# Turning the attention probabilities and half of the LN2 output without TensorE in a DiT block

## The chip, the core and the metric

The kernel runs on one core of a Trainium2 chip. The metric is the device time of one execution in microseconds (us): the median of three runs of the kernel before is 243.12 us (242.97 to 244.42). Engines are named as the profile names them: PE (TensorE, matmuls), PEld (its weight loads), DVE (VectorE), ACT (ScalarE), POOL (GpSimd) and SP (SyncE, which issues most of the DMAs).

## The reference

One block of a diffusion transformer on x of shape (2, 256, 1152), with a modulation vector c of shape (2, 1152), two heads of 576, and a hidden width of 4608, all in bf16:

```python
mod = (silu(c) @ w_mod).reshape(B, 6, 1, D)
shift_a, scale_a, gate_a, shift_m, scale_m, gate_m = [mod[:, i] for i in range(6)]
h = layernorm(x) * (1 + scale_a) + shift_a
q, k, v = split(h @ wqkv)
attn = softmax(einsum('bqhd,bkhd->bhqk', q, k) * Dh ** (-0.5))
x = x + gate_a * (einsum('bhqk,bkhd->bqhd', attn, v).reshape(B, N, D) @ wo)
h2 = layernorm(x) * (1 + scale_m) + shift_m
return x + gate_m * (gelu(h2 @ w_fc1) @ w_fc2)
```

## The kernel before, in words

The 512 tokens are four tiles of 128 (t = 0, 1 for the first batch, 2, 3 for the second); the 1152 features are nine chunks of 128. Weights stream in from DRAM by large DMAs issued on SP. The SBUF is one hand-made arena, and buffers are used again: the four fc1 buffers `WFC1` (512 hidden columns each, so four tiles f) are filled a second time, and the end of the `WFC2` area holds the normalised tiles `XN2` for a while.

Every operation is recorded as a unit with its reads and writes (class `Sched`). Dependencies follow from the regions. The order on PE and on SP is the order in which the code records the units; the order on ACT, DVE and POOL is made by a list scheduler with a cost model (`schedule`), unless `S.first` or `order_after` says otherwise. Each engine then runs its list strictly in order, and an instruction that waits on a semaphore holds up all that stands behind it on that engine. That holds for SP and POOL as issuers of DMAs too.

Stages on PE in order: the modulation columns, k, then q; the scores S of each batch and head, with softmax on DVE and ACT (`s_and_softmax`: maximum, exp with the sum beside it, reciprocal, and a multiplication on DVE at L1013 that normalises the probabilities `PP`); between the v projections (`v_proj`, PSUM banks 0 to 2 in turn) the probabilities are turned (`pt_transposes`: four 128x128 transposes for each batch and head into PSUM, and one copy to `PTS`); `rows` (modulation rows); PV (`pv_halves` for the chunk that the two heads share, then `pv`) into `OT`; the output projection `wo_tile` of t = 0 to 3, with gate, residual and the statistics of LN2. The gate itself is a chain on DVE (`attn_gate`, 18 long operations at L1061 and L1064, run wherever DVE is free) that goes through DRAM (`dit_scratch`).

LN2 gives `XN2[t]`, token-major. `xn2_T(t)` turns it by nine PE transposes into PSUM, from where DVE and ACT write it with scale and shift to `H2T`, feature-major. Then fc1: for the first F0 = 9 of its 36 tiles f, the 256 tokens of batch 0 are computed first (half tiles of nine matmuls of 256 columns), with `xn2_T(2)` after f = 3 and `xn2_T(3)` after f = 6; then the same nine tiles for batch 1; from f = 9 on tiles of 512 columns. ACT applies gelu (L1200). At f = 16, 20, ... the reloaded fc1 quarters are first used. fc2 follows, 13 pieces, each stored as it is done.

SP's order from PV on is: GA loads, fc1 quarters 2 and 3, `WGM` (2592 KB, for the MLP gate), WFC2 parts 1, 2 and 3 (2592 KB each; part 3 must wait until `XN2` has been read), fc1 quarters 4 to 8 (1152 KB each, number 4 needs the buffer of quarter 0 free), WFC2 part 0, output stores.

```python
seq = {e: [u for u in units if u.eng == e] for e in ("pe", "sp")}
...
for f in range(F0, JT):
    if f % 4 == 0 and f // 4 >= 4:
        wfc1_load(f // 4)
    fc1_tile(f, 0, 512)
```

Of the kernel before, what the change touches and what calls it, by code (L numbers as in the profile page):

```python
# [9 lines left out]
SEM_LAT = 120.0  # L10
# [161 lines left out]
class Sched:  # L172
    def __init__(self):
        self.units = []
        self.instrs = []
        self.sb_recs = {}
        self.sb_buckets = defaultdict(set)
        self.bank_pe = defaultdict(list)
        self.bank_other = defaultdict(list)
        self.bank_prev_other = defaultdict(list)  # L180
        self.cur_unit = None
        self.first = {}

# [21 lines left out]

# [75 lines left out]
    def schedule(self, dma_bw=385.0, dma_issue=650.0, dma_lat0=900.0, dma_lat1=600.0, verbose=False):  # L281
# [44 lines left out]
        while scheduled < n:  # L326
# [39 lines left out]
            for f, uid in fin_now:  # L366
                for s in units[uid].succ:
                    ndeps[s.uid] -= 1
                    at = max(avail_time.get(s.uid, 0.0), f + (SEM_LAT if True else 0.0))
# [139 lines left out]
F0 = 9  # L509
# [34 lines left out]
def build_kernel(nc, x, c, wqkv, wo, w_mod, w_fc1, w_fc2, out):  # L544
# [4 lines left out]
    scratch = scratch_t.ap()  # L549
    with (  # L550
# [442 lines left out]
        def s_and_softmax(b, h):  # L993
            idx = b * 2 + h
            bank = s_bank[(b, h)]
            S.unit("pe", 8 * c_mm(256), "S_%d_%d" % (b, h))
            ch = head_chunks[h]
            for jq in range(2):
                for ci, (gq, gk) in enumerate(ch):
                    q0 = b * 256 + jq * 128  # L1000
                    mm(ps32(bank, jq * 256, 256), QK[:, gq, q0:q0 + 128], QK[:, gk, b * 256:(b + 1) * 256], False, ci == len(ch) - 1,
                       skip_group_check=True)
            s3 = ps32(bank).rearrange("p (j k) -> p j k", j=2)
            mx, nb, rsum, ri, pp = MX[:, idx, :], NB[:, idx, :], RS[:, idx, :], RI[:, idx, :], PP[idx]
# [7 lines left out]
            rib = ri.unsqueeze(2).broadcast_to([P, 2, 256])  # L1012
            u = dve(c_dve_tt16(512), lambda e: e.tensor_tensor(out=pp, in0=pp, in1=rib, op=ALU.mult), [pp, ri], [pp], "spn_%d" % idx)  # L1013
            if idx % 2 == 1:
                S.order_after(ga_units[(1, 7) if idx == 1 else (0, 8)], u)

        def pt_transposes(b, h):
            idx = b * 2 + h
            bank = s_bank[(b, h)]
            S.unit("pe", 4 * c_mm(128), "PT_%d_%d" % (b, h))  # L1020
            for kjt in range(2):
                for jq in range(2):
                    tr(ps16(bank, kjt * 256 + jq * 128, 128), PP[idx][:, jq, kjt * 128:(kjt + 1) * 128], IDENT)
            copy_on("dve" if b == 0 else "act", PTS[idx].rearrange("p j k -> p (j k)"), ps16(bank, 0, 512), 512, True, "PT_ev%d" % idx)

        v_banks = [0, 1, 2]
        v_rr = [0]

        def v_proj(t, ci):
            bank = v_banks[v_rr[0] % 3]  # L1030
# [87 lines left out]
        PVB = [(6, 7, 0, 1), (3, 4, 0, 1)]  # L1118

        def pv_halves():  # L1120
            S.unit("pe", 4 * c_mm(256) + 100.0, "PV_halves")
            for b in range(2):
                for kjt in range(2):
                    for h in range(2):
                        f0 = 512 + 64 * h
                        mm(psum[64 * h:64 * h + 64, 5 * 512 + b * 256:5 * 512 + b * 256 + 256], V[:, 2 * b + kjt, f0:f0 + 64],
                           PTS[b * 2 + h][:, kjt, :], b == 0 and kjt == 0, b == 1 and kjt == 1, skip_group_check=True,
                           tile_position=(0, 64 * h))
            S.order_after(copy_on("dve", OT[:, 4, :], ps32(5), 512, False, "OT_ev_4"), last_mt[0])

        def pv(b, h):
# [3 lines left out]
            for g in range(g0, g0 + 4):  # L1135
                bank, half = PVB[b][2 * h + (g - g0) // 2], (g - g0) % 2
                for kjt in range(2):
                    mm(ps32(bank, half * 256, 256), V[:, 2 * b + kjt, g * 128:(g + 1) * 128], PTS[idx][:, kjt, :], kjt == 0, kjt == 1)
            tok = slice(b * 256, (b + 1) * 256)
            for i, eng in ((0, "act"), (1, "dve")):  # L1140
# [12 lines left out]
        def wo_tile(t, before={}):  # L1153
            b = t // 2
            for ci in range(NCH):
# [4 lines left out]
                for g in range(KT):  # L1160
                    mm(o, OT[:, g, t * 128:(t + 1) * 128], WO[:, g, ci * CH:(ci + 1) * CH], g == 0, g == KT - 1)
# [13 lines left out]
        def xn2_T(t):  # L1175
# [7 lines left out]
            for kt in range(KT):  # L1183
                o, dst = slot[kt], H2T[:, kt, t * 128:(t + 1) * 128]
                s1, s2 = SC1M[:, kt * 2 + b:kt * 2 + b + 1], SHM[:, kt * 32 + b:kt * 32 + b + 1]
                if kt < (4 if t < 2 else 6):
# [5 lines left out]

        def fc1_tile(f, tok0, ntok):
# [3 lines left out]
            for kt in range(KT):  # L1197
                mm(o, WFC1[q % 4][:, kt, (f % 4) * 128:(f % 4) * 128 + 128], H2T[:, kt, tok0:tok0 + ntok], kt == 0, kt == KT - 1)
# [23 lines left out]
        pt_transposes(0, 0)  # L1222
        v_proj(1, 0)
        pt_transposes(1, 0)
        v_proj(1, 1)
        v_proj(1, 2)
        pt_transposes(0, 1)
        v_proj(2, 0)
        v_proj(2, 1)
        pt_transposes(1, 1)  # L1230
# [63 lines left out]
        S.n_other_dma_sems = 12  # L1294
# [3 lines left out]
        with ExitStack() as es:  # L1298
            sems = {e: es.enter_context(nc.semaphore("c_" + e)) for e in ENGINES}
            dma_sems = [es.enter_context(nc.semaphore("d%d" % i)) for i in range(60)]  # L1300
# [47 lines left out]
```

## Time and profile before

| what | before |
|---|---|
| median of the timed runs | 243.12 us |
| span of the profiled execution (first to last instruction) | 242.5 us |
| the same execution's own time | the page gives its span alone; the median of the timed runs is 0.6 us longer |
| PE busy | 237.3 us (98%) |
| DVE, ACT, POOL busy | 121.5, 67.8, 19.9 us |
| moved by DMA | 51.58 MB, mean 213 GB/s |

How to read it: the span runs from the first to the last instruction of one profiled execution, and all places in time below are microseconds from its start. The rows of forty digits cut the span into slices of 6.06 us; a digit is a busy share in tenths, and the row PEclk is the clock that TensorE was granted. Matmuls are pipelined and their ends are modelled, so a busy PE in a slice does not mean that it never waited; the chain of waits and the regular distance of the gelu starts (0.98 us for a half tile, 1.94 us for a tile of 512) say that. The landing time of a DMA runs from its issue on SP to its last byte, and holds the time that it stood behind others.

### The profile page before, as it was taken

The page shows a single profiled execution, that of the slowest core. Times are in us where ns is not written, and L with a number is a line of the kernel's source. Part 1 is how long each engine was busy: PE and PEld are TensorE (multiplying, and loading weights), DVE is VectorE, ACT ScalarE, POOL GpSimd, SP SyncE. Part 2 cuts the span into 40 slices and gives each one's busy share as a digit, 9 for nine tenths or more (in the row PEclk, how much of TensorE's full clock was granted, in tenths as well). Part 3 has the DMA queues.
Part 4 walks back from the last instruction along what each step waited for, and adds up shares of the span by engine and source line. Part 5 has one row for each costly group of instructions (what it writes and reads, how often), then busy time and mean ns, then how long its engine had stood idle before and what let it go on. Part 6 is the DMA issues. An engine that isn't in the chain of part 4 may idle for free.

```text
span 242.5 us, 3957 instructions
## 1 busy us (share of the span) xinstructions
PE 237.3 (98%) x1699; PEld 145.4 (60%) x1699; DVE 121.5 (50%) x229; ACT 67.8 (28%) x136; POOL 19.9 (8%) x36
## 2 busy tenths in 40 slices
PE   6899999999999999999999999999999999999995
PEld 2688844466666666898544444444666566566564
DVE  2654379988996689669999700000022222111112
ACT  4921440435524206973233322222000000000000
POOL 1300000000002276400000110000000000000000
PEclk9979999999999999999999999999999999999999
DMA  6999999999992999999963499100000000000000
GB/s 221 378 370 392 389 392 390 398 413 402 391 352 79 312 374 391 391 348 398 352 198 83 157 313 374 43 0 3 0 16 19 16 16 16 19 16 16 21 27 20
DMA packets 30363, 51.58 MB, mean 213 GB/s; under 512 B 1547, under 2 KB 15755, under 8 KB 30347
## 3 DMA queue, kind: packets, MB, share of 16 engines
q1 hardware_dynamic: 29888, 50.73, 58.9%
q0 software_dynamic: 288, 0.60, 0.8%
q8 instruction: 13, 0.21, 0.4%
q10 hardware_dynamic: 171, 0.01, 0.0%
q14 instruction: 3, 0.02, 0.0%
HBM read 50.15 MB, written 1.19 MB: 212 GB/s over the span
## 4 chain that ended last, share of the span: by engine, by line
PE 95%; DMA 3%; SPq 1%; DVE 0%; issue 0%
PE psum L692 93%; DMA arena<-in_wqkv_dram 3%; PE psum L695 2%; SPq L673 1%; DVE arena L1290 0%; DVE arena L1291 0%
## 5 line engine op out<-in xcount | busy, mean ns | idle before, releaser
L692 PE MATMUL psum<-arena 128*128 128x384 bf16 (+8 forms) x1610 | 234.0, 314 | 2.4 <-POOL arena L718 1.5
L692 PEld LDWEIGHTS psum<-arena 128*128 128x128 bf16 (+2 forms) x1610 | 139.7, 97 | 92.4 <-issue 3.8
L1290 DVE TENSOR_TENSOR arena<-psum,arena 128x384 f32<-128x384 f32 (+2 forms) x13 | 6.8, 526 | 88.6 <-PE psum L692 88.6
L1200 ACT ACTIVATE arena<-psum 128x512 bf16<-128x512 f32 (+1 forms) x45 | 22.8, 512 | 42.1 <-PE psum L692 42.1
L687 ACT ACTIVATE arena<-psum 128x512 bf16<-128x512 f32 (+6 forms) x34 | 18.2, 560 | 37.9 <-PE psum L692 37.9
L1064 DVE SCALAR_TENSOR_TENSOR arena<-arena 128x1152 f32<-128x1152 bf16 x16 | 21.9, 1408 | 0.0
L1095 DVE SCALAR_TENSOR_TENSOR arena<-arena 128x1152 f32<-128x1152 bf16 x16 | 21.4, 1414 | 0.0
L1166 POOL TENSOR_TENSOR arena<-arena 128x384 f32<-128x384 f32 x12 | 10.9, 912 | 11.7 <-DVE arena L1165 9.5
L740 DVE BATCH_NORM_STATS2 arena<-arena 128x6 f32<-128x384 f32 (+1 forms) x18 | 9.5, 549 | 3.8 <-DMA arena<-in_x_dram 3.8
L673 POOL DMA_DIRECT2D dit_scratch<-arena x4 | 2.4, 609 | 96.6 <-DVE arena L1082 60.3
L689 DVE CAST arena<-psum 128x512 bf16<-128x512 f32 x11 | 7.2, 687 | 5.3 <-PE psum L692 5.3
L1165 DVE TENSOR_TENSOR arena<-psum,arena 128x384 f32<-128x384 f32 x12 | 6.7, 556 | 3.7 <-PE psum L692 3.7
L1171 ACT ACTIVATE arena<-arena 128x1152 bf16<-128x1152 f32 x4 | 5.4, 1344 | 9.8 <-DVE arena L1170 9.8
L695 PE MATMUL psum<-arena 128*128 128x128 bf16 (+1 forms) x89 | 7.4, 225 | 0.4 <-DMA arena<-in_c_dram 0.4
L695 PEld LDWEIGHTS psum<-arena 128*128 128x128 bf16 (+1 forms) x89 | 6.3, 102 | 2.2 <-DMA arena<-in_c_dram 1.1
L1291 DVE TENSOR_TENSOR arena<-arena 128x384 bf16<-128x384 f32 (+2 forms) x13 | 6.9, 527 | 0.5
L1190 ACT ACTIVATE arena<-psum,arena 128x128 bf16<-128x128 bf16 x16 | 6.1, 455 | 3.0 <-PE psum L695 2.2
L1187 DVE TENSOR_SCALAR arena<-psum,arena 128x128 bf16<-128x128 bf16 x20 | 5.5, 336 | 2.9 <-PE psum L695 2.9
L1009 ACT ACTIVATE arena<-psum,arena 128x256 bf16<-128x256 f32 x8 | 3.7, 471 | 0.2 <-DVE arena L1006 0.2
L744 POOL TENSOR_TENSOR arena<-arena 128x1 f32<-128x1 f32 x6 | 3.3, 555 | 4.7 <-DVE arena L743 4.5
L1005 DVE TENSOR_REDUCE arena<-psum 128x2 f32<-128x512 f32 x4 | 2.8, 688 | 0.9 <-PE psum L692 0.7
L962 ACT ACTIVATE arena<-arena 128x256 bf16<-128x256 bf16 x6 | 2.5, 495 | 1.5 <-DVE arena L956 1.5
(60 smaller groups left out, 53.9 us busy)
## 6 DMA issues: line engine op xcount, KB each, us to landing
arena<-in_w_fc_dram SPq DMA_DIRECT2D x9, 1152.0 KB, 8.0
arena<-in_w_fc_dram SPq DMA_DIRECT2D x4, 2592.0 KB, 17.6
arena<-in_wqkv_dram SPq DMA_DIRECT2D x18, 288.0 KB, 9.3
arena<-in_w_mod_dram SPq DMA_DIRECT2D x6, 864.0 KB, 12.3
arena<-in_w_mod_dram SPq DMA_DIRECT2D x3, 1728.0 KB, 20.5
arena<-in_wqkv_dram SPq DMA_DIRECT2D x1, 2592.0 KB, 17.6
arena<-in_wo_dram SPq DMA_DIRECT2D x1, 2592.0 KB, 24.9
arena<-in_w_mod_dram SPq DMA_DIRECT2D x1, 2592.0 KB, 18.5
```

The lines of the kernel that those rows point to most:

```text
L687: act(c_act(n), lambda e: e.activation(out=dst, in_=src, func=ACTF.Copy), [src], [dst], name)
L689: return dve(c_dve_psum16(n) if psum16 else c_dve_psum32(n), lambda e: e.tensor_copy(dst, src), [src], [dst], name)
L692: S.instr(lambda e: e.matmul(o, lhsT=l, rhs=r, start=st, stop=sp, **kw), reads=[l, r], writes=[o])
L695: S.instr(lambda e: e.transpose(o, i_, idn), reads=[i_, idn], writes=[o])
L740: dve(550, lambda e, s=s, o=o: e.bn_stats(out=o, in_=s), [s], [o], "bn_%s_%d" % (tag, ci))
L1064: ga_units[(b, kt)] = dve(150 + FG * 1.1, lambda e, o=o, w=w, s1=s1: e.scalar_tensor_tensor(out=o, in0=w, scalar=s1, in1=o, op0=ALU.mult, ...
L1095: u = dve(1300, lambda e, o=o, w=w, s1=s1: e.scalar_tensor_tensor(out=o, in0=w, scalar=s1, in1=o, op0=ALU.mult, op1=ALU.add), [w, s1, o], ...
L1165: dve(550, lambda e, o=o, ga=ga, x1c=x1c: e.tensor_tensor(out=x1c, in0=o, in1=ga, op=ALU.mult), [o, ga], [x1c], "wo_t1_%d_%d" % (t, ci))
L1166: S.op("pool", 930, lambda e, xs=xs, x1c=x1c: e.tensor_tensor(out=x1c, in0=x1c, in1=xs, op=ALU.add), reads=[x1c, xs], writes=[x1c], name=" ...
L1200: act(c_act(ntok), lambda e: e.activation(out=dst, in_=o, func=ACTF.Gelu_apprx_tanh), [o], [dst], "gelu_%d_%d" % (f, tok0))
L1290: dve(c_dve_psum32(w), lambda e, o=o, gm=gm, t1=t1: e.tensor_tensor(out=t1, in0=o, in1=gm, op=ALU.mult), [o, gm], [t1], "fc2_t1_%d_%d" % ( ...
L1291: dve(c_dve_32(w), lambda e, t1=t1, x1c=x1c, ost=ost: e.tensor_tensor(out=ost, in0=t1, in1=x1c, op=ALU.add), [t1, x1c], [ost], "fc2_out_%d ...
```

## The change

Three things change.

First, the probabilities. They are normalised by ACT (two activations of 256 for each batch and head) instead of by one DVE multiplication. A DVE block transpose (32x32 blocks, 512 elements in a partition) writes them to `PTF`; a DMA on the POOL queue stores this to DRAM (`p_turn`, 128 KB), and a second DMA on the same queue loads it back with partitions regrouped, in pieces of 256 bytes. The 16 PE transposes and four PSUM copies go. `PTS` is a view of the loaded tile whose columns lie in runs of 32.

Second, LN2. For t = 0 and 1 the PE transposes stay. For t = 2 and 3 DVE turns `XN2[t]` by one block transpose of 1152 elements, SP stores it to DRAM (`h_turn`, 288 KB) and loads it back in pieces of 576 bytes, and nine DVE operations apply scale and shift in place. `H2T` gets a layout in which 32 tokens lie together.

Third, the order. F0 is 14, so 14 tiles f run in halves. The WFC2 parts 1 and 2, which stood before PV in SP's order, now stand behind the two stores and two loads of `h_turn`. The v projections use four PSUM banks, PV has another order and other banks, the copies of PV of batch 0 are all on ACT, `wo_tile` takes chunk 4 last, and the orders of DVE and ACT around softmax are written out.

```diff
+    def in_order(self, eng, names):
+        by_name = {u.name: u for u in self.units if u.eng == eng}
+        for a, b in zip(names, names[1:]):
+            if by_name[a] not in by_name[b].deps:
+                by_name[b].deps.add(by_name[a])
+                self.loose.add((by_name[a].uid, by_name[b].uid))
...
-F0 = 9
+F0 = 14
...
-        H2T = HK
+        H2T = sb(O_HK, 9216).rearrange("p (g k i) -> p k g i", g=16, k=KT)
+        H2F = [sb(O_HK + t * 2304, 2304) for t in range(4)]
...
-        PTS = [sb(O_PT + i * 1024, 1024).rearrange("p (j k) -> p j k", j=2) for i in range(4)]
+        PTF = [sb(O_PT + i * 1024, 1024) for i in range(4)]
+        PTS = [f.rearrange("p (a j t i) -> p t j a i", a=4, j=2, t=2) for f in PTF]
...
-            u = dve(c_dve_tt16(512), lambda e: e.tensor_tensor(out=pp, in0=pp, in1=rib, op=ALU.mult), [pp, ri], [pp], "spn_%d" % idx)
-            if idx % 2 == 1:
-                S.order_after(ga_units[(1, 7) if idx == 1 else (0, 8)], u)
-        def pt_transposes(b, h):
...
+            for jq in range(2):
+                o, aa = pp[:, jq, :], ri[:, jq:jq + 1]
+                act(c_act(256, 1), lambda e, o=o, aa=aa: e.activation(out=o, in_=o, func=ACTF.Copy, scale=aa), [o, aa], [o], "spn_%d_%d" % (idx, jq))
+            src, flat = pp.rearrange("p j (t x c) -> p c (j t) x", t=2, c=4), PTF[idx]
+            u = dve(c_dve_32(512), lambda e: e.transpose(flat, src), [src], [flat], "PT_turn%d" % idx)
+            st, ld = p_turn[idx], p_turn[idx].rearrange("(a x) (c y) -> (x c) a y", a=4, c=4)
+            dma(st, flat, 3 * P * 1024, "st_pt%d" % idx, eng="pool")
+            fl4 = flat.rearrange("p (a y) -> p a y", a=4)
+            dma(fl4, ld, 5 * P * 1024, "ld_pt%d" % idx, eng="pool")
-        v_banks = [0, 1, 2]
+        v_banks = [7, 0, 1, 2]
...
-        PVB = [(6, 7, 0, 1), (3, 4, 0, 1)]
+        PVB = [(6, 7, 0, 1), (2, 5, 7, 0)]
...
-            for i, eng in ((0, "act"), (1, "dve")):
+            for i, eng in ((0, "act"), (1, "dve" if b else "act")):
...
-                for g in range(KT):
+                gs = (0, 1, 2, 3, 5, 6, 7, 8, 4)
+                for g in gs:
...
-                o, dst = slot[kt], H2T[:, kt, t * 128:(t + 1) * 128]
+                o, dst = slot[kt].rearrange("p (g i) -> p g i", i=32), H2T[:, kt, 4 * t:4 * t + 4, :]
...
+        def xn2_turn(t):
+            src, flat = XN2[t].rearrange("p (k x c) -> p c k x", k=KT, c=4), H2F[t]
+            dve(c_dve_32(D), lambda e: e.transpose(flat, src), [src], [flat], "h2turn_%d" % t)
+            dma(h_turn[t], flat, P * D * 2, "st_h2_%d" % t)
+        def xn2_back(t):
+            b, flat = t // 2, H2F[t]
+            dma(flat.rearrange("p (a y) -> p a y", a=4), h_turn[t].rearrange("(a x) (c y) -> (x c) a y", a=4, c=4), P * D * 2, "ld_h2_%d" % t)
+            for kt in range(KT):
+                dst = H2T[:, kt, 4 * t:4 * t + 4, :]
+                s1, s2 = SC1M[:, kt * 2 + b:kt * 2 + b + 1], SHM[:, kt * 32 + b:kt * 32 + b + 1]
+                last_h2T[0] = dve(200, lambda e, dst=dst, s1=s1, s2=s2: e.tensor_scalar(out=dst, in0=dst, scalar1=s1, scalar2=s2, op0=ALU.mult, op1=ALU.add),
+                    [dst, s1, s2], [dst], "h2T_%d_%d" % (t, kt))
...
-        pt_transposes(0, 0)
...
         dma(WGM, wmod_v[:, :, 5 * D:6 * D], D * D * 2, "ld_gm", run=2304)
-        for q4 in range(1, 3):
-            dma(WFC2[:, 9 * q4:9 * q4 + 9, :], wfc2_v[:, 9 * q4:9 * q4 + 9, :], 9 * P * D * 2, "ld_wfc2_%d" % q4, run=2304)
+        pv(0, 0)
+        pv(0, 1)
+        pv(1, 0)
         pv_halves()
-        for b in range(2):
-            for h in range(2):
-                pv(b, h)
+        pv(1, 1)
         wo_tile(0)
...
         wo_tile(3, {2: lambda: xn2_T(1)})
-        for f in range(0, 4):
+        xn2_turn(2)
+        xn2_turn(3)
+        xn2_back(2)
+        xn2_back(3)
+        for f in range(0, F0):
             fc1_tile(f, 0, 256)
-        xn2_T(2)
-        for f in range(4, F0 - 2):
-            fc1_tile(f, 0, 256)
-        xn2_T(3)
-        for f in range(F0 - 2, F0):
-            fc1_tile(f, 0, 256)
+        for q4 in range(1, 3):
+            dma(WFC2[:, 9 * q4:9 * q4 + 9, :], wfc2_v[:, 9 * q4:9 * q4 + 9, :], 9 * P * D * 2, "ld_wfc2_%d" % q4, run=2304)
         dma(WFC2[:, 27:36, :], wfc2_v[:, 27:36, :], 9 * P * D * 2, "ld_wfc2_3", run=2304)
...
+        S.in_order("dve", ga[9:10] + ["smax_0", "snb_0"] + ga[10:11] + ["sri_0"] + ga[11:12] + ["smax_2", "snb_2", "PT_turn0", "smax_1", "snb_1", "sri_2"]
+                   + ga[12:13] + ["smax_3", "snb_3", "sri_1", "PT_turn2"] + ga[13:14] + ["PT_turn1", "sri_3"] + ga[14:15] + ["PT_turn3"] + ga[15:16])
+        S.in_order("act", ["sexp_0_0", "sexp_0_1", "qk_ev8", "spn_0_0", "spn_0_1", "v_ev0_0", "sexp_2_0", "sexp_2_1", "sexp_1_0", "sexp_1_1", "v_ev0_1",
+                           "spn_2_0", "spn_2_1", "spn_1_0", "spn_1_1", "v_ev0_2", "sexp_3_0", "sexp_3_1", "v_ev1_0", "spn_3_0", "spn_3_1", "v_ev1_1", "v_ev1_2"])
```

More of the change, by code (lines that the diff above doesn't have):

```diff
@@ L549, in build_kernel @@
     scratch = scratch_t.ap()
+    p_turn = nc.dram_tensor("p_turn", (4, P, 512), BF16).ap()
+    h_turn = nc.dram_tensor("h_turn", (4, P, D), BF16).ap()
+    TRACK_DRAM.add("p_turn")
+    TRACK_DRAM.add("h_turn")
     with (
@@ L1011, in s_and_softmax @@
             dve(165, lambda e: e.reciprocal(out=ri, in_=rsum), [rsum], [ri], "sri_%d" % idx)
-            rib = ri.unsqueeze(2).broadcast_to([P, 2, 256])
-            u = dve(c_dve_tt16(512), lambda e: e.tensor_tensor(out=pp, in0=pp, in1=rib, op=ALU.mult), [pp, ri], [pp], "spn_%d" % idx)
-            if idx % 2 == 1:
-                S.order_after(ga_units[(1, 7) if idx == 1 else (0, 8)], u)
-        def pt_transposes(b, h):
[L1018 to L1024, printed above, removed]
-        v_banks = [0, 1, 2]
+            for jq in range(2):
[8 more added lines that the diff above has]
+        v_banks = [7, 0, 1, 2]
         v_rr = [0]
         def v_proj(t, ci):
-            bank = v_banks[v_rr[0] % 3]
+            bank = v_banks[v_rr[0] % 4]
             v_rr[0] += 1
@@ L1137, in pv @@
                 for kjt in range(2):
-                    mm(ps32(bank, half * 256, 256), V[:, 2 * b + kjt, g * 128:(g + 1) * 128], PTS[idx][:, kjt, :], kjt == 0, kjt == 1)
+                    mm(ps32(bank, half * 256, 256), V[:, 2 * b + kjt, g * 128:(g + 1) * 128], PTS[idx][:, kjt], kjt == 0, kjt == 1)
             tok = slice(b * 256, (b + 1) * 256)
-            for i, eng in ((0, "act"), (1, "dve")):
+            for i, eng in ((0, "act"), (1, "dve" if b else "act")):
                 g = g0 + 2 * i
@@ L1197, in fc1_tile @@
             for kt in range(KT):
[L1198 removed]
+                mm(o, WFC1[q % 4][:, kt, (f % 4) * 128:(f % 4) * 128 + 128], H2T[:, kt, tok0 // 32:(tok0 + ntok) // 32, :], kt == 0, kt == KT - 1)
             dst = GT[f][:, tok0:tok0 + ntok]
@@ L1299, in build_kernel @@
             sems = {e: es.enter_context(nc.semaphore("c_" + e)) for e in ENGINES}
-            dma_sems = [es.enter_context(nc.semaphore("d%d" % i)) for i in range(60)]
+            dma_sems = [es.enter_context(nc.semaphore("d%d" % i)) for i in range(66)]
             S.emit(nc, block, sems, dma_sems)
```

20 lines of the change are left out of this document (10 added, 10 removed).

## The prediction

> **What bounds the kernel now.** I read the page first, then the chain of waits in order of time, then the SP queue, the stages in windows, and the DMA issues one by one.
>
> ```profile
> span 242.5 us, 3957 instructions
> PE 237.3 (98%) x1699; PEld 145.4 (60%) x1699; DVE 121.5 (50%) x229; ACT 67.8 (28%) x136; POOL 19.9 (8%) x36
> ...
> PEclk9979999999999999999999999999999999999999
> DMA  6999999999992999999963499100000000000000
> ...
> PE 95%; DMA 3%; SPq 1%; DVE 0%; issue 0%
> ```
>
> PE carries 95% of the chain that ended last, so time off PE is time off the kernel as long as PE finds its operands. DMA is saturated from slice 1 to 18, with one gap; so when weights arrive is the second thing to look at. From the chain in order of time:
>
> ```profile
> 67.44 0.22 PE psum L695 x4
> ...
> 96.68 0.50 PE psum L695 x9
> ...
> 102.57 0.50 PE psum L695 x9
> ...
> 106.02 0.50 PE psum L695 x9
> 106.53 133.56 PE psum L692 x810
> ```
>
> Four transposes of one batch and head are 0.22 us of PE, nine of one LN2 tile 0.50, and nothing waits around them. After 106.5 PE never waits again. The DMA issues in short windows (last column: us to landing), and the SP queue's timeline for their times:
>
> ```profile
> arena<-in_w_fc_dram SPq DMA_DIRECT2D x1, 2592.0 KB, 21.0
> ...
> arena<-in_w_fc_dram SPq DMA_DIRECT2D x1, 2592.0 KB, 24.3
> ...
> arena<-in_w_fc_dram SPq DMA_DIRECT2D x1, 1152.0 KB, 8.6
> ...
> arena<-in_w_fc_dram SPq DMA_DIRECT2D x1, 1152.0 KB, 5.5
> ```
>
> These are WFC2 parts 1 and 2 (issued 83.3 and 86.5, landed 104.3 and 110.8), fc1 quarter 4 (112.45, landed 121.05) and quarter 6 (123.2, on an empty queue). Landings go one behind the other: parts 1 and 2 lie 6.5 apart, which is 2.65 MB at 0.39 MB/us; part 3 (11.2 after 106.6, so 117.8) and quarter 4 lie 3.25 apart. Two windows of 2 us show the rate and the idle queue later:
>
> ```profile
> 94.00:96.00 2.00, 2.00 (x14) 1.19 (x13) 2.00 (x7) 2.00 (x4) 0.94 (x2) 1.00 1.05 392
> ...
> 130.00:132.00 2.00, 2.00 (x11) 0.88 (x10) 1.97 (x2) 0.60 (x1) 0.00 (x0) 1.00 0.00 0
> ```
>
> Before, quarter 4 was there at 121.05 and first read at 130.75 (the gelu of f = 15 starts at 130.97, 0.2 behind its matmuls): 9.7 us of slack. This slack is what the change spends.
>
> **The change part by part.**
>
> *PE transposes out.* 4 x 0.22 for the probabilities and 2 x 0.50 for LN2 tiles 2 and 3: 1.88 us less.
>
> *F0 from 9 to 14.* Two half tiles (2 x 0.98 by the gelu starts) take the place of one tile of 1.943 in five more f: 5 x 0.02 = 0.1 more. Net 1.8 less, so without any wait the span would be 240.7.
>
> *Moving operands in runs of 32 columns* (`PTS`, `H2T`). The nearest row is the 72 matmuls of 288 columns of the modulation rows, which read the same runs of 32 and take 2.3 us together (69.1 to 71.4), four at once. No slowing shows: 0. A doubling on the fc1 stage would be some 70 us; I exclude it.
>
> *Softmax on ACT and DVE.* ACT gets 8 x 0.46 (the pitch of L1009) and loses two copies (0.59 each); DVE loses 4 x 0.69 and two copies of 0.42, and gets four block transposes. The nearest rows: 1152 elements f32 1.356, 2304 2.578, so 1.06 ns an element and 0.13 fixed: 0.68 for 512. Walking the written orders from the S stage's own end times, ACT finishes the last normalisation near 63.8 and DVE the last block transpose near 64.6 (before: 65.0 for the normalised tile). A v bank is free 1.5 us or more before its turn. Cover: ACT has 42% idle in 50 to 66.
> The gate chain's last links come about 1.1 later, because its long operations may no longer fill the gap before the first maximum; GA then lands near 82 instead of 81. DVE has 0.15 to 0.9 idle ahead of each gate product of `wo`, so it has caught up before tile 1 ends. I count 0; without that cover it is up to 1.
>
> *Probabilities through DRAM.* Store and load wait in POOL's order, and behind them only the gate's stores (75.2). PV starts at 75.0 now; batch 1, head 1 is first needed by `pv_halves`, 2.6 later, at 77.6. From 64.6 that leaves 13 us for two trips. POOL's own issues take 0.53 to 0.75; its stores of 0.5 to 4 KB landed in 1.6 to 4.0, its loads of 288 KB in 6.5 and 6.7 while SP's queue moved 270 to 370 GB/s. 4 + 6.7 + 2 x 0.7 = 12.1: in time. The other end: if they stand behind all that SP has queued (quarter 1 landed 75.6), the store lands at 75.6 and the load at 82.4, and PE waits 4.8. Below zero there is nothing: the wait can't be shorter than none. I take 0, by the POOL rows, since they sit in a queue of their own on the page (q0).
> The Trainium skill, "DMA: Bandwidth & Descriptors", section Specifications, gives 512 bytes as the least piece for full rate; these loads have 256. No row here shows such pieces; by the skill's page the two trips would take longer, towards the late rival below.
>
> *LN2 tiles 2 and 3.* Before, `XN2[3]` ends at 103.81 (1.33 from 102.48). `wo` comes 0.88 earlier, so 102.95. DVE turns it (1.356) by 104.4; a source with a stride of four elements has no row, between 0 and one more 1.36. The store of 288 KB: output stores of 96 KB land in 1.6, the first GA load of 288 KB in 3.6; I take 2.2 (1.6 and 192 KB at 0.39 MB/us): 106.7. SP then issues the last load (0.35) and is free at 107.2. The load lands at about 110 (3.6 by GA), nine scale-and-shift operations of 0.2 (twelve of 256 elements took 2.44) follow chunk by chunk, and batch 1's half tiles start at 111.3: just in time, with up to 2 us at stake. That wait costs nothing extra if the next step holds.
>
> *WFC2 parts 1 and 2 behind it.* This is the step that decides. SP may not issue 5.3 MB that before were moving from 84 to 108, until 107.2; from about 99 (`WGM` landed 97.5, GA comes 1 later) the DMA engines lie nearly idle. On an empty queue an fc1 quarter (1.18 MB) lands in 5.5; part 1 has 1.47 MB more, at 0.39: 9.3, and 0.5 for the load ahead of it. Landings: part 1 117.0, parts 2 and 3 6.8 behind each other, 130.6, quarter 4 3.3 behind, **133.9**. It is needed after 28 half tiles and two tiles from 97.6: 130.75 - 1.8 = **128.95**. PE waits 5.0. Ends: store 1.6, rate 0.40 and the block transpose earlier give 132; a slow store (3.6), the strided transpose and the lag that long bursts show (parts 1 and 2 land some 3 behind the bytes moved) give 138. So 3 to 9. Quarters 5 to 8 then land 3.2 apart and are needed 7.8 apart: no second wait. WFC2 part 0 and the gate are needed near 175.
>
> *The clock after the wait.* In 7 to 11 PE was busy 3.25 of 4 us; from 11.4 for 3.4 us the granted clock was one half:
>
> ```profile
> 11.00:12.00 1.00, 1.00 (x8) 0.73 (x7) 0.88 (x4) 0.97 (x2) 0.00 (x0) 0.57 1.04 408
> 12.00:14.00 2.00, 2.00 (x11) 1.44 (x10) 1.68 (x4) 0.79 (x2) 0.00 (x0) 0.50 1.05 387
> ```
>
> A wait of 5 us is longer than those gaps. Such a stretch costs up to 1.7, less what of it lies in the wait; I take 0.7.
> The Trainium skill, "TensorE: Matmul & The Clock Gate", Part 1 (the clock gate), says that the clock halves after an idle window of about 3.4 us; the trace agrees in the length of the slow stretch (3.4), and by the skill's rule the 5 us wait would cost between 0 and 1.7 by where the window falls.
>
> **Sum.** 242.5 - 1.8 + 5.0 + 0.7 = 246.4 span; the timed median lies 0.6 above the profiled span: **247.0 us**.
>
> **Rivals.**
> 1. *The turn is free (not slower).* The queue catches up: quarter 4 lands by 128.95. For it: the slack of 9.7 before. Against: the 9.4 MB from 107.2 on (the load, three parts, the quarter) take 22.5 us even at the highest rate in the trace (0.42). It would need the stores to go at 102 or landings out of order. PE's 1.8 stay: 241.3. It decides from 129.
> 2. *A short wait.* Quarter 4 lands before 132.7: 241.3 to 245.5, within 1%.
> 3. *Probabilities late.* PE waits at PV by 2 to 5, the `wo` stage and all behind it shift, the forecast's wait stays: 249 to 252. For it: POOL's order and pieces of 256 bytes; against: 13 us of room.
>
> **How the numbers follow.** Forecast (245.5 to 249.5) 0.60; rival 1 0.08; rival 2 0.15; rival 3 0.14; anything faster than 240.7 0.03, since all of PE's gain is 0.75%. A measurement of this kernel tells about 1% from no change. So faster 0.03, same 0.22, slower 0.75. The range leaves out half of rivals 1 and 2 and part of rival 3: 243.0 to 250.5.
>
> **What would show it.** Eighty-eight L695 matmuls become 54. The GB/s row is near nothing in the slices around 100 to 107. PE's waits name the DMA of in_w_fc_dram, 3 to 9 us, near 129, and the chain that ended last runs through it and back to the h_turn store. The PEclk row dips behind it. Waits of PV on POOL's loads would show rival 3. The prediction is wrong if quarter 4 lands before 129, or if WFC2 moves during 85 to 100.

## The result, and the profile after

| | before | after |
|---|---|---|
| median of the timed runs | 243.12 us | 251.56 us (250.03 to 252.09) |
| ratio after to before | | 1.0337 [1.0310, 1.0364] |
| span of the profiled execution | 242.5 us | 248.3 us |
| PE busy | 237.3 us | 236.4 us |

The change makes the kernel 3.4% slower. The forecast was 247.0 us with a range of 243.0 to 250.5: the sign and the mechanism came as told, the size did not, and the time lies 1.1 us outside the range. The profiled execution of after is its fastest, 250.03 us, so its time lies 1.7 us above its span; the places in time below are from it.

The page of after (busy times; the rows of 40 slices of 6.2 us; the chain that ended last by engine and by line):

```profile
span 248.3 us, 4004 instructions
...
PE 236.4 (95%) x1710; PEld 146.8 (59%) x1710; DVE 123.1 (50%) x233; ACT 69.5 (28%) x143; POOL 25.1 (10%) x44
...
PE   6999999999998999999982999999999999999995
...
PEclk9999999999999999999995899999999999999999
DMA  6999999999996994189999959400000000000000
...
PE 84%; DMA 10%; ACT 2%; DVE 1%; SPq 1%; issue 0%; POOL 0%
```

Before, PE had 95% of the chain and DMA 3%. Now DMA has 10%. The row of PE has one large hole, the 8 and the 2 in slices 21 and 22, where before it was full (the 8 in slice 13 is a smaller one, told below); in slices 22 and 23 PEclk has its 5 and 8. The DMA row shows the same from the other side: it falls to 4 and 1 in slices 16 and 17, where before it was full, and is full in 21 to 23, where before it had 6, 3 and 4.

The chain of waits of after from 100 us (start, duration, what; "issue" is time in which the engine waited for nothing that the profile shows):

```profile
100.47 2.59 ACT arena L1182 x2
103.06 0.28 ACT arena L1225
103.34 0.05 issue
103.38 12.24 PE psum L706 x109
115.62 19.08 DMA arena<-in_w_fc_dram
134.71 0.14 issue
134.84 110.98 PE psum L706 x648
```

The one DMA in it is fc1 quarter 4, issued at 115.62 and landed at 134.7; behind it PE runs to the end without a break. Before, everything from 106.53 on was one piece of PE. What each wait was for (total, times, longest):

```profile
POOL arena L687 <- DMA p_turn<-arena: 9.9, 2, 5.7
...
PE psum L706 <- DMA arena<-in_w_fc_dram: 5.5, 1, 5.5
...
PE psum L706 <- ACT arena L701: 1.2, 1, 1.2
```

The 5.5 is the wait at f = 16. By the regular distance of the gelu starts PE was ready at 129.1, so 5.7 us went. The 1.2 is a second wait, at the start of PV (74.2 to 75.4). ACT is named because its copies ended at 75.28; but the load of the probabilities of batch 0, head 1 landed at 75.25, so this trace can't tell the two apart. In the first experiment below the same wait names the load:

```profile
PE psum L706 <- DMA arena<-p_turn: 1.3, 1, 1.3
```

Before, PE ran through PV without a wait, in one piece from 67.67 to 93.25:

```profile
67.67 25.59 PE psum L692 x229
```

Three of the SP transfers that decide, each from a short window around its issue (last column: us from issue to landing):

```profile
arena<-in_w_fc_dram SPq DMA_DIRECT2D x1, 2592.0 KB, 10.2
...
arena<-in_w_fc_dram SPq DMA_DIRECT2D x1, 2592.0 KB, 22.9
...
arena<-in_w_fc_dram SPq DMA_DIRECT2D x1, 1152.0 KB, 19.1
```

WFC2 part 1 (issued 107.1) landed at 117.3, part 3 (108.4) at 131.3, quarter 4 (115.6) at 134.7. The prediction had 117.0, 130.6 and 133.9. The windows of after around the wait (busy us and instructions of PE, PEld, DVE, ACT, POOL, then granted clock, DMA share, GB/s):

```profile
100.00:102.00 2.00, 2.00 (x21) 1.79 (x19) 0.49 (x4) 1.53 (x2) 0.76 (x2) 1.00 0.03 8
...
130.00:132.00 2.00, 0.00 (x0) 0.00 (x0) 2.00 (x2) 0.00 (x0) 0.00 (x0) 0.85 1.10 351
132.00:134.00 2.00, 0.00 (x0) 0.00 (x0) 2.00 (x3) 0.00 (x0) 0.00 (x0) 0.50 1.10 348
134.00:136.00 2.00, 1.16 (x3) 0.44 (x4) 1.97 (x2) 0.00 (x0) 0.00 (x0) 0.50 1.10 349
136.00:138.00 2.00, 2.00 (x6) 0.76 (x5) 1.97 (x2) 0.00 (x0) 0.00 (x0) 0.50 1.10 349
138.00:140.00 2.00, 2.00 (x10) 0.85 (x9) 2.00 (x1) 0.60 (x1) 0.00 (x0) 0.94 1.10 347
```

At 100 to 102 the DMA engines move 8 GB/s where before they were full with WFC2 parts 1 and 2: the queue is idle while LN2 is turned. At 130 to 134 PE does nothing and DMA is at its rate, the reverse of before (0 GB/s, PE full). And the clock is one half from 131.4 to 138.2, so that the tile f = 16 takes 3.6 us (134.84 to 138.45, 0.2 before its gelu) where 1.94 is usual: 1.7 us are lost after the wait has ended.

One sign of the prediction came only in part: the chain runs through quarter 4, but from its issue at 115.62 back into PE, and not to the store of `h_turn`.

### The profile page after: what moved, and what is told of

Read it like the earlier page. It is cut to its first block, busy times and chain, and to the rows that moved or that the text cites. A ratio compares the mean times of both kernels' runs of the same rounds, so it can differ in the third digit from the quotient of the medians.

```text
span 248.3 us, 4004 instructions
## 1 busy us (share of the span) xinstructions
PE 236.4 (95%) x1710; PEld 146.8 (59%) x1710; DVE 123.1 (50%) x233; ACT 69.5 (28%) x143; POOL 25.1 (10%) x44
## 4 chain that ended last, share of the span: by engine, by line
PE 84%; DMA 10%; ACT 2%; DVE 1%; SPq 1%; issue 0%; POOL 0%
PE psum L706 83%; DMA arena<-in_w_fc_dram 8%; DMA arena<-in_w_mod_dram 3%; ACT arena L1182 1%; SPq L687 1%; PE psum L709 1%; DVE arena L754 1%; ACT arena L701 0%; POOL arena L758 0%; DVE arena L1176 0%; DVE arena L845 0%; ACT arena L1225 0%; DVE arena L1310 0%; DVE arena L1311 0%; DVE arena L1181 0%
## 5 line engine op out<-in xcount | busy, mean ns | idle before, releaser
L706 PEld LDWEIGHTS psum<-arena 128*128 128x128 bf16 (+2 forms) x1655 | 143.6, 97 | 97.1 <-issue 11.5
L1225 ACT ACTIVATE arena<-psum 128x256 bf16<-128x256 f32 (+1 forms) x50 | 23.4, 476 | 50.5 <-PE psum L706 50.4
L701 ACT ACTIVATE arena<-psum 128x512 bf16<-128x512 f32 (+5 forms) x34 | 18.0, 559 | 32.9 <-PE psum L706 32.8
L703 DVE CAST arena<-psum 128x512 bf16<-128x512 f32 x9 | 6.0, 687 | 6.9 <-PE psum L706 6.9
L687 POOL DMA_DIRECT2D p_turn<-arena x4 | 2.4, 600 | 39.5 <-DVE arena L1030 39.5
L1215 DVE TENSOR_SCALAR arena<-arena 128x128 bf16<-128x128 bf16 x18 | 4.1, 308 | 3.7 <-DMA arena<-h_turn 3.7
L709 PE MATMUL psum<-arena 128*128 128x128 bf16 (+1 forms) x55 | 4.2, 218 | 0.5 <-DMA arena<-in_c_dram 0.5
L709 PEld LDWEIGHTS psum<-arena 128*128 128x128 bf16 (+1 forms) x55 | 3.5, 97 | 1.8 <-DMA arena<-in_c_dram 1.4
L1201 ACT ACTIVATE arena<-psum,arena 128x128 bf16<-128x128 bf16 x10 | 3.8, 453 | 2.2 <-PE psum L709 2.2
L687 POOL DMA_DIRECT2D arena<-p_turn x4 | 3.0, 762 | 9.9 <-DMA p_turn<-arena 9.9
```

The source lines that it names most:

```text
L687: return S.op(eng, 500.0 if eng == "sp" else 150.0, lambda e: e.dma_start(dst, src), reads=[src], writes=[dst], name=name, dma_bytes=nbyte ...
L701: act(c_act(n), lambda e: e.activation(out=dst, in_=src, func=ACTF.Copy), [src], [dst], name)
L706: S.instr(lambda e: e.matmul(o, lhsT=l, rhs=r, start=st, stop=sp, **kw), reads=[l, r], writes=[o])
L709: S.instr(lambda e: e.transpose(o, i_, idn), reads=[i_, idn], writes=[o])
L1225: act(c_act(ntok), lambda e: e.activation(out=dst, in_=o, func=ACTF.Gelu_apprx_tanh), [o], [dst], "gelu_%d_%d" % (f, tok0))
```

## The experiments

The theory after this reading: WFC2 parts 1 and 2, put behind the `h_turn` trip, push fc1 quarter 4 past its first reader; that wait and the half clock behind it are nearly the whole loss. The rivals: the probabilities' trip, the layout in runs of 32 columns or the fourteen half tiles cost something by themselves; or the DMA engines have too much to move wherever it stands in the queue. The times of before beside the runs were 243.04 to 243.11 us.

### Only the place of WFC2 part 3, and parts 1 and 2 back in their old place

The first edit leaves everything of the change as it is and gives quarter 4 a shorter queue: part 3 (first needed near 175) goes behind quarter 5.

```diff
-        dma(WFC2[:, 27:36, :], wfc2_v[:, 27:36, :], 9 * P * D * 2, "ld_wfc2_3", run=2304)
         mlp_gate(last_h2T[0])
...
                 wfc1_load(f // 4)
+            if f == 20:
+                dma(WFC2[:, 27:36, :], wfc2_v[:, 27:36, :], 9 * P * D * 2, "ld_wfc2_3", run=2304)
             fc1_tile(f, 0, 512)
```

> The changed kernel with one DMA moved: WFC2 part 3 is issued behind fc1 quarter 5 instead of ahead of quarter 4. Queue theory (quarter 4 late by 5.7 us behind three WFC2 parts, and 1.9 us of half clock after that wait, are nearly the whole loss): quarter 4 lands right behind part 2, near 128, ahead of the 129.1 at which it is needed; no wait at f = 16 and no dip of the clock there; span 248.3 - 7.6 = 240.7, time 241 to 243.5. Probabilities theory (the trips of the probabilities through DRAM are the loss) and layout theory (runs of 32 columns and 14 half tiles make PE slower): nothing changes by more than 1.5, time 249 or more.

Measured: 243.16 us, ratio 0.9999 [0.9987, 1.0011]. The 8.4 us of loss are gone with one line moved. Its fc1 quarter 4 in the DMA issues, and the end of its chain of waits:

```profile
arena<-in_w_fc_dram SPq DMA_DIRECT2D x1, 1152.0 KB, 12.2
```

```profile
103.61 0.28 ACT arena L1225
103.93 135.17 PE psum L706 x864
```

Issued at 116.3, quarter 4 lands at 128.5, about 1.3 ahead of its need (129.8 in this execution, which runs 0.55 later from the start), and from 103.9 PE runs in one piece, as before. Its granted clock is 1.00 throughout. (The expectation puts 1.9 on the half clock after the wait; the trace of after has 1.7, since the 0.2 from the matmuls to the gelu belong to every tile.) So neither the layout nor the half tiles nor the bytes are the loss; the order of the queue is.

The second edit is the other way to undo the move: WFC2 parts 1 and 2 go back ahead of PV, as they stood in before.

```diff
         dma(WGM, wmod_v[:, :, 5 * D:6 * D], D * D * 2, "ld_gm", run=2304)
+        for q4 in range(1, 3):
+            dma(WFC2[:, 9 * q4:9 * q4 + 9, :], wfc2_v[:, 9 * q4:9 * q4 + 9, :], 9 * P * D * 2, "ld_wfc2_%d" % q4, run=2304)
```

(and the same two lines leave their place behind the loads of `h_turn`).

> The changed kernel with WFC2 parts 1 and 2 issued ahead of PV again, as in the kernel before. Queue theory: the parts flow from 92 to 112, the h_turn stores and loads stand behind them in the same queue and land near 112 and 115, so the wait moves from f = 16 to the first half tile of batch 1: 3 to 5 us there (and up to 1.7 of half clock), none at f = 16; time 245 to 249. Probabilities or layout theory: 249 or more, with no wait of 3 us at the first half tile of batch 1 that names h_turn.

Measured: 250.71 us, ratio 1.0305 [1.0267, 1.0343], more than expected. The quarter is in time now, but the turn itself is late. The end of its chain of waits:

```profile
103.97 8.24 DMA h_turn<-arena
112.22 2.75 DMA arena<-h_turn
115.00 2.33 DVE arena L1215 x10
117.37 128.91 PE psum L706 x792
```

The store of 288 KB takes 8.2 us (2.1 on the idle queue of after): it is issued at 104.0, and WFC2 part 2, ahead of it in the same queue, lands only at 111.5. The first half tile of batch 1 waits 5.2 us for its operand. Its windows show the clock again, one half from 114.5 to 121.3; 3.9 us of this lie behind the wait and cost 2.0, where the expectation had up to 1.7:

```profile
114.00:116.00 2.00, 0.00 (x0) 0.00 (x0) 1.00 (x5) 0.00 (x0) 0.00 (x0) 0.62 0.97 286
116.00:118.00 2.00, 0.63 (x3) 0.31 (x3) 2.00 (x10) 0.00 (x0) 0.00 (x0) 0.50 0.95 328
118.00:120.00 2.00, 2.00 (x11) 1.11 (x11) 2.00 (x7) 0.38 (x1) 0.00 (x0) 0.50 1.03 354
120.00:122.00 2.00, 2.00 (x14) 1.56 (x13) 2.00 (x3) 0.38 (x1) 0.00 (x0) 0.68 1.03 399
```

So the move of parts 1 and 2 was no careless one: with the turn going through DRAM, 5.3 MB stand either ahead of the turn or ahead of quarter 4, and each costs about as much. Of the orders tried here, only the one in which part 3, with 2.65 MB, gives way fits both.

### Each part alone

The probabilities' part put into the kernel before, and nothing of LN2:

> The kernel before with only the part of the probabilities (ACT normalisation, block transpose, two POOL DMAs, v banks, PV order); LN2 tiles 2 and 3 stay on PE, F0 = 9, WFC2 order as before. Queue theory: PE loses 0.9 and waits up to 1.5 for the loads at PV; quarter 4 keeps its slack; time 242.0 to 244.0. Probabilities theory: 246 to 251.

Measured: 243.45 us, 1.0013 [1.0000, 1.0027]. The sixteen transposes are gone (0.9 us) and nothing is won, because PE waits at PV:

```profile
PE psum L703 <- DMA arena<-p_turn: 1.1, 1, 1.1
```

The LN2 part put into the kernel before (with the fourteen half tiles and the moved WFC2 parts), and nothing of the probabilities:

> The kernel before with only the LN2 part (block transpose and h_turn trips for tiles 2 and 3, F0 = 14, the new H2T layout, WFC2 parts behind the trips); the probabilities stay on PE. Queue theory: quarter 4 lands as late as in the changed kernel, PE waits 5 to 7 us at f = 16 and then runs at half clock for some us; time 249.5 to 252.5. Probabilities theory: 244 or less.

Measured: 251.12 us, 1.0335 [1.0279, 1.0392]. This is the loss of the whole change, with the same wait:

```profile
PE psum L695 <- DMA arena<-in_w_fc_dram: 5.6, 1, 5.6
```

The LN2 part alone with part 3 behind quarter 5, the edit of the first experiment:

> e4_ln2_only (probabilities on PE) with WFC2 part 3 behind fc1 quarter 5. Queue theory: no wait at f = 16; PE loses the 1.0 us of two LN2 turns, pays 0.1 for five more half tiles and 0.4 to 0.7 for gelu behind two LN2 activations in a row and for the first half tile of batch 1; time 242.4 to 243.0. Layout theory: above 244.

Measured: 243.40 us, 1.0017 [1.0001, 1.0034]; 0.4 to 1.0 more than expected. The gelu starts lie 0.98 apart up to 111.66, and the next is at 113.74: the first half tile of batch 1 came 1.1 late. In DVE's timeline the scale-and-shift operations start behind the load (start, duration, instruction, and the idle time before it with what ended it):

```profile
109.26 4.10 DVE L1207 TENSOR_SCALAR arena<-arena 128x128 bf16<-128x128 bf16 x18 [4.57 <-DMA arena<-h_turn]
```

In after they start at 108.20 and the half tile is only 0.25 late. (The store of tile 2 takes 3.0 us here and 2.1 in after; why isn't known.) This is the "just in time, with up to 2 us at stake" of the prediction, seen on both of its sides.

### The order in POOL's queue

The wait at PV can be followed in POOL's timeline of after, where the stores and loads of the probabilities are issued:

```profile
54.13 0.76 POOL L687 DMA_DIRECT2D p_turn<-arena  x1 [39.53 <-DVE arena L1030]
60.59 0.78 POOL L687 DMA_DIRECT2D arena<-p_turn  x1 [5.70 <-DMA p_turn<-arena]
61.37 1.62 POOL L687 DMA_DIRECT2D p_turn<-arena  x3
67.23 2.25 POOL L687 DMA_DIRECT2D arena<-p_turn  x3 [4.24 <-DMA p_turn<-arena]
```

The first load stands second in POOL's list. It waits 5.70 us for the first store to land, and behind it stand three stores whose data had been ready at 57.9, 59.8 and 61.8. They go out together at 61.4 to 63, their loads at 67.2 to 69.5, and these take 6 to 7 us. The list scheduler had put the load there. The edit writes the order out, on top of the first experiment: all stores, in the order in which the data become ready, then all loads.

```diff
+        S.first["pool"] = ['ones', 'nhalf', 'gba0', 'ident', 'c_silu32', 'rstd_ln1_1', 'rstd_ln1_0', 'rstd_ln1_2', 'rstd_ln1_3', 'st_pt0', 'st_pt2', 'st_pt1', 'st_pt3', 'ld_pt0', 'ld_pt2', 'ld_pt1', 'ld_pt3']
         S.schedule()
```

> e1_part3_last with the POOL queue in another order: the four stores of the probabilities first, then the four loads (before, the first load waited in POOL for the first store to land and held the other three stores back until 61). If POOL's order makes the loads late, stores 2, 1 and 3 go at 58, 60 and 62, the loads by 67.5, the PV wait of 1.3 us goes, and the time is 241.7 to 242.3. If the trips themselves are too long (5.5 and 7.3 us each beside the weight stream), 0.8 us or more of the wait stays and the time is 242.7 to 243.3.

Measured: 241.70 us (241.57 to 242.27), ratio 0.9946 [0.9933, 0.9959]. **This version beats both kernels**: 1.4 us (0.6%) faster than before, 9.9 faster than after. Its POOL timeline:

```profile
54.48 0.76 POOL L687 DMA_DIRECT2D p_turn<-arena  x1 [39.78 <-DVE arena L1030]
58.54 0.55 POOL L687 DMA_DIRECT2D p_turn<-arena  x1 [3.31 <-DVE arena L1030]
60.45 0.54 POOL L687 DMA_DIRECT2D p_turn<-arena  x1 [1.35 <-DVE arena L1025]
62.43 0.54 POOL L687 DMA_DIRECT2D p_turn<-arena  x1 [1.44 <-DVE arena L1030]
62.96 0.79 POOL L687 DMA_DIRECT2D arena<-p_turn  x1
```

The second store goes at 58.54 instead of 61.4, each wait of a store is now for DVE's data, and no wait of PE is left at PV. From the first experiment to this one it is 1.46 us.

The same order alone, once on the probabilities' part in the kernel before, once on after as it is:

> e3_probs_only with the four stores ahead of the four loads in POOL. POOL's order as the cause of the PV wait: 1.1 us less than e3_probs_only, 242.1 to 242.6, so that PE's 0.9 shows at last. If the trips are too long anyway: 243.0 to 243.5.

> The changed kernel with only the POOL order of e5_stores_first; WFC2 part 3 stays ahead of quarter 4. Queue theory: the turn of XN2[3] follows PE, so the h_turn trips, the WFC2 parts and quarter 4 all come 1.3 us earlier, the wait at f = 16 stays 5 to 6 us, and the time is 249.5 to 250.8. If quarter 4's landing doesn't follow PE: 251 to 252, with a longer wait.

Measured: 242.41 us (0.9973 [0.9963, 0.9984]; 1.04 less than with the scheduler's order) and 250.21 us (1.0298 [1.0279, 1.0316]; 1.35 less than after). In the second the wait at f = 16 stays:

```profile
PE psum L706 <- DMA arena<-in_w_fc_dram: 5.9, 1, 5.9
```

Counted from the first store of the probabilities (54.13 in after, 54.96 here), PE comes to f = 16 1.3 us earlier than in after and quarter 4 lands 0.9 earlier, since its place in time follows PE's through LN2 and the trip. That is why the two losses add up, all but 0.4, instead of hiding one behind the other.

Last, whether the small pieces make these trips long. On top of the version above the loads go in pieces of 1024 bytes instead of 256; the regrouping of the partitions, and with it the right order of the probabilities, is left out.

```diff
-            dma(fl4, ld, 5 * P * 1024, "ld_pt%d" % idx, eng="pool")
+            dma(flat, st, 5 * P * 1024, "ld_pt%d" % idx, eng="pool")
```

> e5_stores_first with the loads of the probabilities in pieces of 1024 bytes instead of 256; the regrouping of partitions is left out, so the probabilities that PV reads are not the turned ones. If the small pieces make a load long, it lands in 5.4 us or less, like the stores (5.0 to 5.4, also 1024-byte pieces). If the weight stream beside it does, it still lands in 6.0 to 7.5. Span 239.5 to 240.5 in both cases.

Measured, in a single execution: 242.02 us; the four loads landed in 5.3, 5.3, 5.4 and 6.9 us where they had taken 6.0, 6.0, 6.3 and 7.5. So the pieces, or the regrouping that goes with them, cost 0.6 to 0.9 of each load, and the time of the kernel gains nothing without them. The rest, above 5 us for 128 KB, is there with large pieces too. It comes while SP's stream moves some 390 GB/s. A pair of small stores on POOL points to that stream: the gate's stores of 4 and 0.5 KB landed in 5.4 and 5.1 us in after, beside it, and in 1.8 and 1.6 in before, where they were issued at 75.2 and 75.9 and quarter 1, the last of the stream, landed at 75.6. The Trainium skill, "DMA: Bandwidth & Descriptors", section Specifications, puts the least piece for full rate at 512 bytes; these rows agree that 256 is slower, by about a tenth of the load.

### The clock by itself

In after, 25 matmuls whose result nobody reads are put between f = 15 and f = 16, so that PE is busy during the wait. They take 5.4 us and end before quarter 4 lands.

```diff
+            if f == 16:
+                for i in range(25):
+                    S.unit("pe", 215.0, "fill_%d" % i)
+                    mm(ps32(0), GT[0][:, 0:128], GT[0], True, True)
```

> The changed kernel with 25 matmuls of 512 columns on PE between f = 15 and f = 16 that write an unused PSUM bank (5.4 us of PE work in the wait, of which nothing is used). If the half clock after the wait costs 1.7 to 3.4 us: mean clock 1.0 instead of 0.986, quarter 4 as late as before, time 248.0 to 249.8 and less spread between runs. If the clock costs nothing: time 251 to 252.

Measured: 249.54 us (249.12 to 249.77), ratio 1.0268 [1.0252, 1.0284], 2.0 less than after. The quarter is as late as before (its chain has 19.25 us for it, and PE starts at 135.60), but the windows keep the clock:

```profile
134.00:136.00 2.00, 1.70 (x9) 0.62 (x7) 1.97 (x3) 0.00 (x0) 0.00 (x0) 1.00 1.10 348
136.00:138.00 2.00, 2.00 (x11) 0.90 (x10) 2.00 (x1) 0.26 (x1) 0.00 (x0) 1.00 1.10 349
```

Eleven matmuls in 136 to 138 stand against six in after. So by the medians the wait costs 6.4 us (249.54 less the 243.16 of the first experiment), and what it does to the clock 2.0 more. In the traces, each of the fastest of its four executions, the two are 5.7 (after) or 5.9 (here, 129.7 to 135.6) and 1.7. The times of this kernel also spread over 0.65 us only, those of after over 2.06.

### Nine half tiles instead of fourteen

> The changed kernel with F0 = 9 instead of 14, all else the same. Queue theory: the landing of quarter 4 sets the end, so the wait only moves: about 4 us at the first half tile of batch 1 (h_turn load and scale-and-shift until about 112), little at f = 16, which still starts near 135; time 248 to 251.5, the lower end if the clock no longer dips behind f = 16. If the half tiles or their number cost the time: below 247.

Measured: 249.83 us, 1.0272 [1.0252, 1.0292]. The time is inside what was expected, but not by the way that was expected. Quarter 4 is issued at 118.35 and lands at 135.3; PE comes to f = 16 only at 136.6 (the gelu of f = 15 starts at 136.86), and none of its waits names `in_w_fc`. PE lost its time earlier:

```profile
PE psum L706 <- DVE arena L1198: 1.8, 2, 1.3
PE psum L706 <- DVE arena L1215: 1.6, 1, 1.6
PE psum L706 <- ACT arena L1225: 0.7, 1, 0.7
```

With five fewer half tiles of batch 0 the need of `H2T` for batch 1 comes 4.9 us earlier; that is the second line (L1215 is the scale-and-shift behind the loads of `h_turn`). The other two lines lie between 98 and 105. There the orders of ACT and DVE, which the list scheduler makes, are other ones than in after: the first gelu starts at 104.7, behind both LN2 activations, where after has it at 99.1, ahead of them. So this edit of one line changed more than the number of half tiles. Behind the wait of 1.6 us, and a first half tile that took 2.0 us instead of 0.98, the granted clock is one half for 3.4 us, from 113.2 to 116.6:

```profile
112.00:116.00 4.00, 4.00 (x20) 2.32 (x20) 4.00 (x11) 0.39 (x2) 0.00 (x0) 0.65 1.05 402
```

The run therefore says nothing for or against a quarter 4 that sets the end; the first experiment and the filled wait carry that. It does show what the fourteen half tiles are for: with nine of them the turn of LN2 is late.

## Why the prediction was right and wrong, step by step

The terms of the sum beside what the runs gave (medians; the whole is 251.56 less the 243.11 of before beside the later runs):

| step | predicted | measured | from |
|---|---|---|---|
| PE transposes and half tiles | -1.8 | -1.8 | what is left of 241.70 - 243.11 = -1.41 without the row below |
| order of ACT around LN2, first half tile of batch 1 | not priced | +0.4 | trace of the version with the stores first |
| probabilities through DRAM | 0 | +1.46 | first experiment less stores first |
| wait for quarter 4 | +5.0 | +6.38 | filled wait less the first experiment |
| half clock | +0.7 | +2.02 | after less the filled wait |
| sum | +3.9 | +8.45 | |

The rows are differences between neighbouring versions, so they must add up to the whole, and the first one is a remainder. On other versions the order of POOL's queue is worth 1.04 (probabilities alone) and 1.35 (after). The +0.4 are 0.27 that PE's matmuls miss at 102.6, where a gelu behind two LN2 activations holds a PSUM bank, and 0.13 at the first half tile of batch 1.

**Right.** *PE transposes out* and *F0 from 9 to 14*: 89 matmuls of that line became 55, the 34 that were told (its 88 and 54 are one short each), and -1.8 holds, as far as a remainder can show it. *Moving operands in runs of 32 columns* cost nothing: the pitch of the gelu starts is 0.98 and 1.94 as before. *Softmax on ACT and DVE* cost nothing; the block transposes took 0.71 for 512 elements (0.68 predicted), and the bf16 source of 1152 elements with a stride of four took 1.36, so the doubling that was held open didn't come. *The gate chain*: GA landed at 81.9 and 83.9, 1.3 and 1.5 later than before and near what was told, but that is luck. DVE's last link (L1092, L1082 before) came 2.2 us earlier than before (1.8 of it is the shift told below), not 1.1 later; the two stores on POOL then took 5.4 and 5.1 us instead of 1.8 and 1.6. The cover was enough, as told: in the version with the stores first the chain that ended last runs through the gate, and PE waits 0.1 for it at 94.4. *LN2 tiles 2 and 3* were just in time, 0.25 late in after. *WFC2 parts 1 and 2 behind it* was the step that decides, by the mechanism and with landings 0.3 to 0.8 from those worked out. (Its 6.5 us for 2.65 MB is 0.41 MB/us, not the 0.39 told; the sum went on with 6.8, and after had 7.2 and 6.8.) Rivals 1 and 2, a free turn and a short wait, are out: the queue didn't catch up.

**Wrong, first: the clock after the wait (0.7, measured 2.0 in the medians, 1.7 in the trace).** The step took one half-clock stretch of 3.4 us, part of it inside the wait. The windows show 6.8 us, twice as long: half clock starts at 131.4, 2.3 us into the wait, and lasts until 138.2, 3.4 us after PE starts again. So only the first half lies in the wait and the second is paid in full. Three more traces have such a wait, and half clock went on for 3.9 us (parts 1 and 2 ahead of PV), 3.3 (the LN2 part alone) and 3.1 (the stores first on after) once PE had started again. All four timed executions of after have the granted clock of 0.986 that this trace has. The Trainium skill, "TensorE: Matmul & The Clock Gate", Part 1, has the clock return only after a busy window of about 3.4 us; the 3.4 us from 134.8 to 138.2 agree, and an estimate by that rule would have been 1.7 once the clock has fallen, not a share of it. The fall itself came 2.3 us into the wait, sooner than the idle window of about 3.4 us that the prediction took from the same part of the Trainium skill; there the measurement decides.

**Wrong, second: probabilities through DRAM (0, measured 1.46).** The step reckoned one store and one load in a row, 12.1 us in 13 of room. It left out POOL's order: the first load holds three stores back by up to 3.5 us. A load took 5.8 to 7.3 and a store 5.6 to 6.2, where 6.7 and 4 were counted. The load that was late is that of batch 0, head 1, where the step had reckoned with batch 1, head 1 alone: its data were ready at 59.8, PE wanted it at 74.2, and it landed at 75.25, 15.5 us behind its data; in the version with the stores first the same trip takes 11.7 (60.45 to 72.12). Rival 3 had the place, with POOL's order named for it, and a price (2 to 5) somewhat above what came; the pieces of 256 bytes, its other reason, cost 0.6 to 0.9 of a load that the right order hides. That the time lies inside rival 3's 249 to 252 is in part luck: its own price was too high, and the wait and the clock were too low.

**Wrong, third: the wait for quarter 4 (5.0, measured 6.4).** In the profiled execution it is 5.7: quarter 4 landed 0.8 later than worked out, and PE was there 0.15 later. The other 0.7 is the difference between this execution, the fastest of the four, and the median one; that one has no trace. Its granted clock is the same 0.986, so the half-clock stretch was as long; whether quarter 4 landed later there isn't shown.

**The base of the sum.** The step added 0.6 to the span to get to the median. The time lies 1.7 to 1.8 above the span in every timed execution of every kernel here. The profiled execution of before was unlike most: it had the half-clock stretch at 11 to 15 us that the prediction showed, and a granted clock of 0.993. Of 19 executions of before beside the first experiment one has that clock and a span of 242.6; the others have 1.0 and spans of 241.0 to 241.7. The two errors cancel in the sum (242.5 + 0.6 and 241.4 + 1.7). But the places in time moved: the 150th matmul starts at 18.94 in before's trace and at 17.18 in after's, and from there on PE is 1.8 us earlier, so a place of the one trace can't be set beside a place of the other as it stands.

**Why the range missed.** Forecast and rival 3 were given chances as if one excluded the other, so that the upper end was set near the forecast's own end. They are losses at two places of one chain, and they came together. The top of the forecast (249.5) with the least of rival 3 (2) is 251.5, within 0.1 of the time; a range worked out from such sums would have reached that far.

## What to carry to other kernels

When a transfer that others wait for must pass through a queue of large weight loads, each load behind it is late by all that stands ahead; so price every moved load at its first reader, and let the one with the latest reader give way (part 3 here, 2.65 MB with a reader over 40 us later, turned +3.4% into none). In an issuing engine's list a load that waits for its own store holds back the stores behind it: issue all the stores first. The waits of 5 to 6 us on PE cost 1.5 to 2.0 us of half clock on top here, and the waits of 1.1 to 1.4 us at PV none; where the limit lies wasn't tested. And the costs of two waits on one chain are added, not chosen between.

## What the runs showed of the hardware that was not expected

- After a wait of 5.7 us the granted clock was one half for 6.8 us, 3.4 of them after work had begun again; filling the wait with unused matmuls of the same kind kept it at 1.00 and gave 2.0 us back. In the kernel with the WFC2 parts ahead of PV the same followed a wait of 5.2 us (114.5 to 121.3). With nine half tiles, a wait of 1.6 us with a slow half tile behind it was followed by 3.4 us of half clock (113.2 to 116.6).
- A DMA of 128 KB issued on POOL took 5.0 to 7.5 us beside SP's saturated stream. One of 288 KB issued on SP took 2.1 to 3.2 in after, on idle engines, and 8.2 where WFC2 part 2 stood ahead of it in its own queue.
- DVE's block transpose of bf16 takes the same time per element as the f32 rows predicted (1.36 us for 1152), with a source stride of four elements too.
- A half-clock stretch at 11 to 15 us of the kernel is there in the traces of before and of the probabilities alone, and not in the other eleven. By the granted clock of 0.993, 1 of 19 timed executions of before has one as well, and that one is 1.3 us above their median: a profiled execution can carry such a stretch and its median not.
